# First unit's x made by products with parts of the identity instead of transfers, more warming products, and a new step plan

## The chip, the cores and the metric

The kernel runs on one core of one Trainium2 chip. The metric is the device time of one execution in microseconds (us); lower is better. Five engines matter: TensorE (PE, matrix products), VectorE (DVE), ScalarE (ACT), GpSimd (POOL) and SyncE (SP, which issues most transfers).

## The reference

A gated linear recurrence for every batch and head, followed by a two-layer network. All inputs of the recurrence are float32; `w_in` and `w_out` come out as float64, so the kernel receives them as pairs of 32-bit words.

```python
# q, k, v, f_logit: (4, 8, 768, 48)
f = 1 / (1 + exp(-f_logit))
for t in range(S):
    state = f[:, :, t, :, None] * state + einsum('bhd,bhe->bhde', k[:, :, t], v[:, :, t])
    y[:, :, t] = einsum('bhd,bhde->bhe', q[:, :, t], state)
x = y.transpose(0, 2, 1, 3).reshape(3072, 384)      # tokens by heads*dims
h = x @ w_in                                        # 384 x 2048
g = h * (1 / (1 + exp(-1.702 * h)))
out = g @ w_out                                     # 2048 x 384
```

## The kernel before

**Units.** The 3072 tokens are worked in twelve units of 256 tokens (three for each batch entry). For a unit the recurrence is solved in chunks of 64 tokens: f, q and k are loaded and turned so that head dimensions lie on partitions; six levels (block sizes 1 to 32) each make score products on PE (`score`, L448), multiply the q and k halves by running products of f in place on DVE (`promote`, L542 or L546), set a copy of K aside on ACT (`set_aside`, Kc, L517) and move the masked scores into the matrix A (`evacuate`, L489, L498, L508). The next level's score needs the Kc and the promoted q of the level before. Then K is turned (`turn_k`, tkn L621, kn L622), chunk states are formed (pd L669 on PE; L691 to L695 on DVE), y is summed in PSUM from A times v (`add`, L558) and from the states times q (L716), and the part "W" brings y to x.

**From y to x.** y lies in PSUM as 48 rows for each of two heads (partitions 0 to 47 and 64 to 111) and four head pairs. The network wants x with 128 of the 384 features on partitions, three such blocks. `half(h)` copies y into the tile yT on ACT (L731) and `to_x` moves it into xT by transfers (L781, L786): for units 0 and 1 the second half goes partly through ACT's queue, else all are on SP's. The first 96 features of each block are two heads of one pair; the last 32 of each come from the fourth pair.

**Network.** Units 0 and 1 work by `mlp_block`: for four of the sixteen 128-wide slices of the hidden layer at a time, four h steps (`mlp_h`, L1130, three products each, then the gelu on ACT into g, L1134) and eight o steps (`mlp_o`, L1144; summed by L1194 or L1196). Later units use other product schemes (L897, L1036). These steps form one list, `fill`, and each plan letter "f" emits the next one.

**Weights.** `pairs` holds sixteen pieces of weights. `fetch_weights` (L207) issues the transfer of a piece's words into one of three buffers (bits). `begin_pair` scales its high words on ACT in place (L239) and queues three DVE steps: low (L235), high (L228, which needs the scaled high words) and both (L238, the result into w_in or w_out). `convert` emits one queued step. A fetch reuses the buffer of the piece three before it. Piece numbers 0 and 1 are w_in, 2 and 3 w_out, and so on by fours. An h or o step stands in the list with the count of pieces that it needs done.

**Order.** Until the end of unit 2's plan every engine's order is the program's order, written by hand. `opening` does unit 0, and part of unit 1's loads and turns. Then `follow(n, fill, PLAN[n])` emits the parts of unit n in turn, and after each part the letters of its entry:

```text
f  next fill step          c  one convert step       p  begin the next piece
w  fetch a piece           s  a sum of weights       k  keep_up: one 128x320 product of the
HOLES: letters inside unit 2's levels                   identity with masks, result unused
```

The first part of unit 1 is composed: unit 0's part "W" (y L716 and then x), followed by unit 1's level 0. PE and DVE thus meet unit 0's y, its x, and then unit 1's first scores in this order. `bank` hands out four PSUM banks in turn to products that need one.

**Start.** A table load on ACT, the clearing of A on DVE (L121), then two warming products on the cleared A (L116), the POOL work for the identity and masks, and the turns of unit 0's f, k and q on PE (L379) with copies on ACT (L384).

Of the kernel before, what the change touches and what calls it, by code (L numbers as in the profile page):

```python
# [23 lines left out]
def kernel(  # L24
# [96 lines left out]
    nc.vector.memset(A, 0.0)  # L121
    nc.vector.memset(ones, 1.0)
    serial = count()
    flat_A = A.rearrange("p c f t -> p (c f t)")
    keep_up(2, 192, (flat_A[:, :P], flat_A[:, :192]))

    R = U // 32
    RW = R * D + HS - D
# [42 lines left out]
    D2, DR = 2 * D, P - 2 * D  # L171
    assert NP == NK + 1 and NK * DR == D2

    NGR = NFF // FG


# [14 lines left out]
    R_BY_ACT = range(0)  # L191
    fetched, todo = {}, []
    state = {"fetch": 0, "begin": 0, "done": 0, "behind": 0}

# [15 lines left out]
    def begin_pair(m):  # L210
# [14 lines left out]

        def high():
            t["s"] = tmp("s", 1).bitcast(I32)
            ve.tensor_scalar(t["s"], hi, 3, None, op0=ALU.logical_shift_left)  # L228

        def low():  # L230
            t["r"] = tmp("a", 2).bitcast(I32)
            if m in R_BY_ACT:
                nc.scalar.activation(t["r"], lo.bitcast(U32), AF.Copy, scale=2.0 ** -29)
            else:
                ve.tensor_scalar(t["r"], lo.bitcast(U32), 2.0 ** -29, None, op0=ALU.mult)  # L235
# [4 lines left out]
        if m in R_BY_ACT:  # L240
            low()
        else:
            todo.append(low)
        todo.extend((high, both, None))

    def begin_next():

        if state["begin"] < len(pairs):
            begin_pair(state["begin"])
            state["begin"] += 1  # L250

    def convert():
# [77 lines left out]
    def rows(h):  # L330
        return slice(h * HS, h * HS + D)
# [6 lines left out]
    def attention(n):  # L338
# [211 lines left out]
        def add():  # L550


            t["py"] = ps.tile([P, NG, NP, 2, HS], F32, tag="y", name=f"y_{n}")
            for a in range(NP):
                for f in (1, 0):
                    for h, g in TILES:
                        to, w = (slice(0, HS), HS) if h == g == 0 else (columns(h, g), D)
# [141 lines left out]
        def _():  # L699
# [614 lines left out]
    def opening():  # L1314

        begin_f, begin, begin_k, begin_gates = units[0][0]
        next_f, next_q, next_k, next_gates = units[1][0]
        level, evacuate, turn_k = units[0][2]
        load_raw(0, 0)
        load_raw(0, 2)  # L1320
        load_raw(0, 1, (nc.scalar,))
        fetch_weights()
        begin_f()
        begin_gates()
        begin_k()
        begin()
        load_raw(1, 0)
        load_raw(1, 2)
        load_v(0)
        load_raw(1, 1)  # L1330
        fetch_weights()
        fetch_weights()
        for l in range(NL):
            chosen[:] = [2, 3][l % 2:][:1]
            level(l)
            if l in (2, 3):
                next_f((0, 4)[l - 2:][:1])
            elif l < NL - 1:
                keep_up(1)
            if l == 1:  # L1340
                begin_pair(0)
                state["begin"] = 1

        nc.scalar.activation(q_end, q_end, AF.Gelu_apprx_sigmoid)
        chosen[:] = [2, 3]
        turn_k(0)
        turn_k(2)
        for l in range(NL - 1):
            evacuate(l)
            if l == 1:  # L1350
                units[0][3]()
        chosen[:] = [2, 3, 2, 3]
        next_q()
        begin_pair(1)
        state["begin"] = 2
        evacuate(NL - 1)
        units[0][1][-2][1]()
        next_gates()
        for _ in range(NOP):
            convert()  # L1360
        fetch_weights()

    fill = []
    opening()
    FIRST = 'k'
# [13 lines left out]
    fill += mlp_blocks((0, 0)) + mlp_blocks((0, 1))  # L1379
    fill += mlp_blocks((1, 0), (1, 1)) + mlp_blocks((0, 2), (1, 2)) + mlp_blocks((0, 3), (1, 3))  # L1380
    follow_steps(FIRST)
    follow(1, fill, PLAN[1])
    chores += [*sums_of_w(("c3", "p15", "c2", "p6"))]
    follow(2, fill, PLAN[2])
    assert state["fetch"] == len(pairs)
    fill_order.close()
    assert state["done"] == 2 * len(pairs) or moe_w_in.dtype == F32
    while chores:
        chores.pop(0)()
    for n in range(N_FILL, NALL):  # L1390
# [46 lines left out]
```

## Time and profile before

| | |
|---|---|
| three runs | 585.39, 586.55, 587.39 us; median 586.55 |
| profiled execution | 586.86 us; its span 585.1 us, first to last instruction |
| busy: PE, DVE, ACT, POOL | 566.7, 442.3, 289.3, 141.7 us |
| keep-up and warming products (L116) | 28 instructions |
| first h product of the network (L1130) | 40.48 us from the span's start |
| transfers into xT for unit 0 | issued 34.20 to 37.58 us |
| unit 1's y products (L716) | start at 64.16 us |

Every matrix product in float32 shows as two matmul instructions. All later times in a trace count from the start of the span. The rest of the device time, 1.76 us, lies outside the span.

### The profile page before, as it was taken

The numbers are of one execution on the slowest core, as the hardware profiler recorded it, in microseconds if no ns is written. First come the engines' busy times: TensorE is split into PE (matmuls) and PEld (weight loads), VectorE is DVE, ScalarE is ACT, GpSimd is POOL, SyncE is SP. The second block draws the span as 40 slices with busy tenths as digits, with TensorE's granted clock in tenths as the row PEclk, the third lists the DMA queues.
The fourth block names the chain that finished last, engine by engine and source line by source line (L and its number), as shares of the span: only waits on it lengthen the run. The fifth ranks groups of instructions, "written<-read, shape, count | busy, mean of one in ns | idle before, by whom it ended". The sixth has DMA issues, their size and how long they took to land.

```text
span 585.1 us, 18537 instructions
## 1 busy us (share of the span) xinstructions
PE 566.7 (97%) x7838; PEld 516.1 (88%) x7838; DVE 442.3 (76%) x697; ACT 289.3 (49%) x588; POOL 141.7 (24%) x226
## 2 busy tenths in 40 slices
PE   7989899999999999999999999999999999999997
PEld 6757676776889999999999999999999999998896
DVE  1899887996888886997786897786897786461284
ACT  4755544322543563663563563564563563552440
POOL 3030120605442601501501601502502503103000
DMA  7869695932453362362443353452451211001000
GB/s 184 192 167 240 151 258 132 241 79 71 104 137 75 103 148 59 97 154 68 122 117 69 93 135 89 111 128 59 120 130 43 64 39 29 29 2 30 26 1 29
DMA packets 86772, 60.34 MB, mean 103 GB/s; under 512 B 33505, under 2 KB 78465, under 8 KB 86689
## 3 DMA queue, kind: packets, MB, share of 16 engines
q1 hardware_dynamic: 86208, 58.57, 40.2%
q8 instruction: 62, 1.02, 0.7%
q10 hardware_dynamic: 481, 0.59, 0.4%
q14 instruction: 21, 0.17, 0.1%
HBM read 45.49 MB, written 8.91 MB: 93 GB/s over the span
## 4 chain that ended last, share of the span: by engine, by line
PE 67%; DVE 12%; DMA 9%; ACT 5%; SPq 3%; issue 2%; POOL 0%; ACTq 0%; DVEq 0%; POOLq 0%
PE h L1036 14%; PE o_Y L897 12%; PE o_Z L897 9%; PE sc L448 6%; PE h_y L1036 5%; PE o_X L897 5%; DMA bits<-in_moe_w_in_dram 4%; PE o_W L897 4%; PE h L1130 3%; PE o L1144 3%; DVE X L367 2%; PE y L716 2%; DMA raw<-in_q_dram 2%; PE sc L669 2%; DVE z L629 2%
## 5 line engine op out<-in xcount | busy, mean ns | idle before, releaser
L546 DVE TENSOR_TENSOR X<-X,tot 128x1024 f32<-128x1024 f32 x50 | 67.2, 1345 | 45.3 <-PE sc L448 37.4
L517 ACT COPY Kc<-X 128x512 f32<-128x512 f32 x72 | 48.2, 670 | 86.2 <-DVE X L546 66.2
L998 POOL TENSOR_TENSOR E<-xT 128x128 f32<-128x128 f32 (+1 forms) x36 | 17.1, 484 | 228.0 <-DMA xT<-yT 228.0
L1130 PE MATMUL h<-xT,w_in 128*128 128x256 f32 x288 | 66.1, 383 | 3.8 <-DMA xT<-yT 2.9
L1130 PEld LDWEIGHTS h<-xT,w_in 128*128 128x128 f32 x288 | 53.5, 190 | 14.0 <-issue 4.0
L1036 PE MATMUL h<-E,w_in 128*128 128x128 f32 (+1 forms) x476 | 62.8, 277 | 0.6 <-DVE g L1064 0.6
L1036 PEld LDWEIGHTS h<-E,w_in 128*128 128x128 f32 x476 | 57.4, 192 | 1.5 <-issue 0.9
L897 PE MATMUL o_Y<-T,S 128*128 128x192 f32 x320 | 57.7, 329 | 0.0
L1066 ACT ACTIVATE g<-g 128x512 f32<-128x512 f32 (+1 forms) x70 | 40.3, 589 | 28.3 <-DVE g L1064 28.2
L897 PEld LDWEIGHTS o_Y<-T,S 128*128 128x128 f32 x320 | 52.2, 190 | 0.6
L1064 DVE TENSOR_TENSOR g<-g,h 128x512 f32<-128x512 f32 (+1 forms) x58 | 35.9, 638 | 16.3 <-PE h L1036 14.8
L367 DVE STREAM_TRANSPOSE X<-raw 128x512 f32<-128x512 f32 x40 | 42.9, 1111 | 3.1 <-PE y L716 2.7
L1144 PE MATMUL o<-w_out,g 128*128 128x384 f32 x128 | 43.7, 491 | 0.1
L508 DVE COPY_PREDICATED A<-masks,sc 128x256 f32<-128x256 uint32 (+1 forms) x98 | 41.8, 504 | 0.1
L1144 PEld LDWEIGHTS o<-w_out,g 128*128 128x128 f32 x128 | 23.7, 190 | 14.8 <-issue 0.2
L731 ACT COPY yT<-y 48x256 f32<-48x256 f32 (+1 forms) x66 | 21.1, 370 | 29.3 <-PE y L716 28.9
L394 POOL TENSOR_SCALAR F<-F 128x1024 f32<-128x1024 f32 x10 | 12.3, 1228 | 87.6 <-ACT F L397 87.6
L1055 ACT ACTIVATE g<-h 128x512 f32<-128x512 f32 (+1 forms) x52 | 28.5, 576 | 9.6 <-PE h L1036 9.3
L448 PE MATMUL sc<-X,Kc 48*64 48x64 f32 x1344 | 28.1, 220 | 2.7 <-ACT Kc L517 1.1
L448 PEld LDWEIGHTS sc<-X,Kc 48*64 48x64 f32 x1344 | 24.0, 134 | 6.9 <-ACT Kc L517 3.1
L897 PE MATMUL o_X<-w_out,g 128*128 128x192 f32 x160 | 29.6, 331 | 0.5 <-ACT o_X L861 0.5
L1134 ACT ACTIVATE g<-h 128x256 f32<-128x256 f32 x48 | 17.2, 383 | 24.9 <-PE h L1130 24.7
(161 smaller groups left out, 1201.8 us busy)
## 6 DMA issues: line engine op xcount, KB each, us to landing
bits<-in_moe_w_out_dram SPq DMA_DIRECT2D x8, 768.0 KB
raw<-in_f_logit_dram SPq DMA_DIRECT2D x48, 96.0 KB
raw<-in_k_dram SPq DMA_DIRECT2D x48, 96.0 KB
bits<-in_moe_w_in_dram SPq DMA_DIRECT2D x8, 576.0 KB
raw<-in_q_dram SPq DMA_DIRECT2D x44, 96.0 KB
k_tok<-z SPq DMA_DIRECT2D x64, 64.0 KB
kt<-k_tok SPq DMA_DIRECT2D x16, 256.0 KB
out_dram<-osb SPq DMA_DIRECT2D x20, 192.0 KB
```

Source lines behind the costliest of these rows:

```text
L367: nc.vector.transpose(view(out, at, [[HALF, NP], [step, R4], [R4 * step, 32]]), by_half[:, j, f].rearrange("p a (j d) -> p (a j) d", j=R4) ...
L448: nc.tensor.matmul(t["sc"][h][g * HS:(g + 1) * HS, a, s, :], lhsT=t["Kc", l][rows(h), x:x + HS], rhs=rhs(h, a, g), start=True, stop=True,)
L508: moved = nc.vector.copy_predicated(out=view(A, c * HALF + at, dims), mask=mask.bitcast(U32), data=got)
L517: nc.scalar.copy(c.rearrange("p (n two m) -> p n two m", two=2, m=m), view(X, KF * SLOT, [[2 * m, SLOT // (2 * m)], [(KR - KF) * SLOT + m, ...
L546: nc.vector.tensor_tensor(x, x, y, ALU.mult)
L897: nc.tensor.matmul(t[name], lhsT=lhs(f), rhs=rhs(f), start=(new and i == 0), stop=(i == HF - 1), skip_group_check=True,)
L1036: nc.tensor.matmul(ph[:, t], lhsT=WA[a][:, f // 2, f % 2 * P:(f % 2 + 1) * P], rhs=E[n][b], start=(root and t == 0), stop=not goes_on, ski ...
L1055: nc.scalar.activation(to, ph, AF.Copy, scale=float(sign))
L1064: copied["sum"] = nc.vector.tensor_tensor(to, to, part, ALU.add if sign > 0 else ALU.subtract)
L1066: nc.scalar.activation(to, to, AF.Gelu_apprx_sigmoid)
L1130: nc.tensor.matmul(ph, lhsT=w_in[:, ff // 2, c, ff % 2 * P:(ff % 2 + 1) * P], rhs=xTs[n][:, c, :], start=(c == 0), stop=(c == NK - 1))
L1144: nc.tensor.matmul(t["po"], lhsT=g[ff // FG][:, ff % FG, tt * P:(tt + 1) * P], rhs=w_out[:, ff, :], start=(ff == ffs[0]), stop=(ff == ffs[ ...
```

## The change

1. **Start.** The warming products go from two to six, and the clearing of A is split: the 192 columns that they read first, the rest behind them.
2. **Parts of the identity.** The unused place of `w_out[:, 15, :128]` first holds `select`, two groups of identity columns copied by POOL: heads' rows 0 to 47 and 64 to 111 side by side (96 columns), and 32 columns for the middle block.
3. **Unit 0's x.** y of unit 0 is placed so that a head's rows stay the same for both token groups (`columns`, `add`). Two copies (one per direction f) bring 112 rows of y into yT; three pairs of products with `select` or `ident` (96 and 32 rows of output) write x into two PSUM banks; two copies bring them into xT. No transfer is left for unit 0.
4. **Plan.** New letters: "a" begins a piece whose low word is scaled by ACT instead of DVE, "i" a small product of the identity with itself. "f" now converts until its piece is done, "w" does nothing where no buffer is due, and a begin fetches a piece that isn't fetched. The conversion of piece 0 is spread over the opening. PLAN and HOLES are new; the opening's places for letters are listed in `PLAN[0]`.

```diff
-    nc.vector.memset(A, 0.0)
+    serial = count()
+    WARM = 6
+    flat_A = A.rearrange("p c f t -> p (c f t)")
+    nc.vector.memset(flat_A[:, :192], 0.0)
+    keep_up(WARM, 192, (flat_A[:, :P], flat_A[:, :192]))
+    nc.vector.memset(flat_A[:, 192:], 0.0)
     nc.vector.memset(ones, 1.0)
-    keep_up(2, 192, (flat_A[:, :P], flat_A[:, :192]))
...
+    select = w_out[:, NFF - 1, :P]
+    nc.gpsimd.tensor_copy(select[:, :D2]..., view(ident, 0, [[HS, 2], [1, D]]))
+    nc.gpsimd.tensor_copy(select[:, D2:]..., view(ident, DR, [[DR, 2], [1, DR // 2]]))
...
-    HOLES = {(N_FILL, 0): "ccp", (N_FILL, 1): "cwcc", (N_FILL, 2): "cwp", (N_FILL, 3): "cc", (N_FILL, 4): "cw"}
+    HOLES = {(N_FILL, 0): "wc", (N_FILL, 1): "ckccc", (N_FILL, 2): "fcp", (N_FILL, 3): "cc", (N_FILL, 4): "pwcw"}
...
         def columns(h, g):
-            return rows(h ^ g)
+            return rows(h ^ g if n else h)
...
+            if not n:
+                for f in (1, 0):
+                    at, step = (0, 1) if f else (U - 1, -1)
+                    nc.scalar.copy(
+                        view(yT[:HS + D], at, [[U, NP], [step * HS, NG], [step, HS]]),
+                        py[:HS + D].rearrange("p g a f t -> p f a g t")[:, f],
+                    )
+                to = [bank([P, 2, U], "x_0"), bank([P, 1, U], "x_1")]
+                for c in range(NK):
+                    pt = to[c // 2][:, c % 2]
+                    y = yT[:HS + D].rearrange("p a g t -> p a (g t)")
+                    nc.tensor.matmul(pt[:D2], lhsT=select[:HS + D, :D2], rhs=y[:, c], start=True, stop=True)
+                    rest = (ident[:HS + D, :DR], select[:HS + D, D2:], ident[:HS + D, HS + DR // 2:HS + D])[c]
+                    nc.tensor.matmul(pt[D2:], lhsT=rest, rhs=y[:, NK], start=True, stop=True)
+                    if c:
+                        nc.scalar.copy(xT[:, 2 * c - 2:c + 1, :], to[c // 2])
+                xTs[n] = xT
+                return
...
             if step == "f":
-                assert fill[0][2] <= state["done"], (fill[0], state)
+                while fill[0][2] > state["done"]:
+                    convert()
                 fill.pop(0)[1]()
...
+            elif step == "a":
+                begin_next(True)
+            elif step == "i":
+                keep_up(1, P, (ident, ident))
             elif step == "w":
-                fetch_weights()
+                if state["fetch"] < min(len(pairs), state["done"] // 2 + PAIRS_AHEAD):
+                    fetch_weights()
...
     PLAN = {
         3: (
-            "fffffffsffsf", "fsffsffsf", "f", "fsfsfsffsfsfsf", "", "ffff", "ff", "ffffffffffffffffsffsf", "fffsf",
+            "fcfffffffff", "sfsffsfsfsf", "", "fsffsffssfsfsf", "", "fffff", "fffffff", "fffffffffffsfffspfa",
+            "fffs",
         ),
+        0: (
+            "ik", "k", "kpc", "ck", "k", "", "", "k", "", "", "", "", "", "", "", "", "", "", "ckw",
+        ),
         1: (
-            "cccwcccwkkkkk", "kkkcf", "cfccwf", "fcffcwffcffcf", "ffcc", "f", "cwc", "fcc", "ffcf", "pw", "fw", "ff",
+            "pcccckkwccwff", "f", "kcfccccwf", "ffcfwfkfccf", "ffcc", "f", "wcwc", "ccf", "ffcf", "", "fw", "ff",
             "fffffff",
         ),
         2: (
-            "ffff", "ffffffff", "fcfcfcwffcfcfcwfffcfcfcff", "sss", "fcfcfcfffffss", "fcfcfcffffffff", "",
-            "fffffffffff",
+            "ffff", "fffffffff", "fcfccfwffcffcpfccfcwfcffa", "sss", "fcffcfffcffss", "fafccfffffffafff", "p",
+            "ffffffffff",
         ),
     }
```

In the opening the letters of `PLAN[0]` stand behind the turns of f (entry 1), the products of f and the turns of k (2), the turns of q (3), each of the six levels (4 to 9), the turning of K (10), the moves of five levels (11 to 15), unit 1's q (16), the last move (17), the states (18) and unit 1's products of f (19). Before, there were keep-ups behind levels 0, 1 and 4, `begin_pair(0)` behind level 1, `begin_pair(1)` behind unit 1's q, and three convert steps, a fetch and a keep-up at the end.

More of the change, by code (lines that the diff above doesn't have):

```diff
@@ L172 @@
     assert NP == NK + 1 and NK * DR == D2
+    select = w_out[:, NFF - 1, :P]
+    nc.gpsimd.tensor_copy(select[:, :D2].rearrange("p (h d) -> p h d", h=2), view(ident, 0, [[HS, 2], [1, D]]))
+    nc.gpsimd.tensor_copy(select[:, D2:].rearrange("p (h d) -> p h d", h=2), view(ident, DR, [[DR, 2], [1, DR // 2]]))
     NGR = NFF // FG
@@ L190 @@
     NOP = 3
-    R_BY_ACT = range(0)
     fetched, todo = {}, []
@@ L244, in begin_pair, with begin_next @@
         todo.extend((high, both, None))
-    def begin_next():
+    def begin_next(by_act=False):
         if state["begin"] < len(pairs):
-            begin_pair(state["begin"])
+            if state["fetch"] == state["begin"]:
+                fetch_weights()
+            begin_pair(state["begin"], by_act)
             state["begin"] += 1
@@ L556, in add @@
                     for h, g in TILES:
-                        to, w = (slice(0, HS), HS) if h == g == 0 else (columns(h, g), D)
+                        to, w = (slice(0, HS), HS) if h == 0 and (not n or g == 0) else (columns(h, g), D)
                         nc.tensor.matmul(
@@ L1337, in opening @@
                 next_f((0, 4)[l - 2:][:1])
[L1338 to L1342, printed above, removed]
+            follow_steps(next(places))
         nc.scalar.activation(q_end, q_end, AF.Gelu_apprx_sigmoid)
@@ L1351, in opening @@
                 units[0][3]()
+            follow_steps(next(places))
         chosen[:] = [2, 3, 2, 3]
         next_q()
-        begin_pair(1)
-        state["begin"] = 2
+        follow_steps(next(places))
         evacuate(NL - 1)
+        follow_steps(next(places))
         units[0][1][-2][1]()
+        follow_steps(next(places))
         next_gates()
-        for _ in range(NOP):
-            convert()
-        fetch_weights()
+        follow_steps(next(places))
     fill = []
-    opening()
-    FIRST = 'k'
     PLAN = {
         3: (
-            "fffffffsffsf", "fsffsffsf", "f", "fsfsfsffsfsfsf", "", "ffff", "ff", "ffffffffffffffffsffsf", "fffsf",
+            "fcfffffffff", "sfsffsfsfsf", "", "fsffsffssfsfsf", "", "fffff", "fffffff", "fffffffffffsfffspfa",
[3 more added lines that the diff above has]
+            "ik", "k", "kpc", "ck", "k", "", "", "k", "", "", "", "", "", "", "", "", "", "", "ckw",
         ),
         1: (
-            "cccwcccwkkkkk", "kkkcf", "cfccwf", "fcffcwffcffcf", "ffcc", "f", "cwc", "fcc", "ffcf", "pw", "fw", "ff",
+            "pcccckkwccwff", "f", "kcfccccwf", "ffcfwfkfccf", "ffcc", "f", "wcwc", "ccf", "ffcf", "", "fw", "ff",
             "fffffff",
@@ L1380 @@
     fill += mlp_blocks((1, 0), (1, 1)) + mlp_blocks((0, 2), (1, 2)) + mlp_blocks((0, 3), (1, 3))
-    follow_steps(FIRST)
+    opening()
     follow(1, fill, PLAN[1])
@@ L1384 @@
     follow(2, fill, PLAN[2])
-    assert state["fetch"] == len(pairs)
+    while state["done"] < 2 * len(pairs):
+        convert()
     fill_order.close()
-    assert state["done"] == 2 * len(pairs) or moe_w_in.dtype == F32
     while chores:
```

14 lines of the change are left out of this document (9 added, 5 removed).

## The prediction

> **What bounds the kernel now.** I read the busy shares first, then who TensorE (PE) waits for, then the opening on PE and VectorE (DVE) in order of time, because the diff touches only the opening and the step plans of units 1 to 3. Line 1 of the page and the longest of PE's waits:
>
> ```profile
> PE 566.7 (97%) x7838; PEld 516.1 (88%) x7838; DVE 442.3 (76%) x697; ACT 289.3 (49%) x588; POOL 141.7 (24%) x226
> ```
> ```profile
> PE h L1130 <- DMA xT<-yT: 2.9, 2, 1.8
> PE idle L116 <- DVE A L121: 2.0, 1, 2.0
> PE sc L448 <- ACT Kc L517: 1.1, 2, 0.8
> ...
> PE h L1130 <- ACT g L1134: 0.8, 1, 0.8
> ...
> PE sc L448 <- DVE A L508: 0.6, 1, 0.6
> ```
>
> PE is the bound. It has 18.4 us of idle, and busy time that is worth nothing: the keep-up products "idle" (L116). The opening shows both, as does the timeline of PE:
>
> ```profile
> 2.02 1.65 PE L116 MATMUL idle<-A 128*128 128x192 f32 x4 [2.02 <-DVE A L121]
> 4.47 8.32 PE L379 MATMUL t<-ident,raw 128*64 128x128 f32 x96 [0.81 <-DMA raw<-in_q_dram]
> ...
> 31.64 1.04 PE L716 MATMUL y<-X,st 48*48 48x64 f32 x46 [0.22 <-ACT y L680]
> ...
> 33.15 2.96 PE L116 MATMUL idle<-masks,ident 128*128 128x320 f32 x10
> 36.90 0.71 PE L448 MATMUL sc<-X,Kc 48*64 48x64 f32 x32 [0.79 <-ACT Kc L517]
> 37.53 1.88 PE L116 MATMUL idle<-masks,ident 128*128 128x320 f32 x6
> 40.48 1.88 PE L1130 MATMUL h<-xT,w_in 128*128 128x256 f32 x6 [1.06 <-DMA xT<-yT]
> 42.29 0.69 PE L448 MATMUL sc<-X,Kc 48*64 48x64 f32 x32
> ```
>
> Unit 0's y ends at 32.7; its first product h starts at 40.48. Between them PE does two score products of unit 1 (L448) and eight keep-ups. From 40.48 on it is dense. The remaining idle before 130 us is 1.83 at 69.5 (unit 1's xT transfers), 0.35 at 77.4 (Kc), 0.60 at 83.8 (L508) and 0.81 at 127.7 (g).
>
> DVE in the same stretch does the weight conversion (L235, L228, L238) between unit 1's levels (L542):
>
> ```profile
> 30.43 1.32 DVE L235 TENSOR_SCALAR a<-bits 128x768 int32<-128x768 uint32 x1
> ...
> 33.64 1.42 DVE L542 TENSOR_TENSOR X<-X,F 128x512 f32<-128x512 f32 x2
> 34.98 0.68 DVE L489 TENSOR_TENSOR A<-sc,masks 128x512 f32<-128x512 f32 x1
> 35.58 0.55 DVE L235 TENSOR_SCALAR a<-bits 128x768 int32<-128x768 uint32 x1
> ```
>
> It has no idle time from 30.4 to 50.6: while x travels, DVE converts pairs 1 and 2 and finishes unit 1's level 0. That cover is what the change disturbs.
>
> **The start.** The clearing of A before the warming products is cut from 1024 to 192 columns (0.91 us, so about 0.25), and they start near 1.3 instead of 2.02. There are twelve instructions instead of four. They follow one another by 0.32 us, so they end near 5.3, after the raw f that PE waited for at 4.47. The turns L379 ran slowly first and fast later, with the granted clock (PEclk, third from the end) at 1.00 in both stretches of the windows view, PE's busy time and count standing ahead:
>
> ```profile
> 4.50:10.00 5.50, 5.50 (x52) 5.50 (x54) 1.00 0.92 236
> 10.50:12.50 2.00, 2.00 (x40) 2.00 (x38) 1.00 0.90 207
> ```
>
> That is 0.106 us an instruction, then about half (0.055 between starts); the change of pace came 5.8 us into the unbroken work that began at 4.47. If unbroken work from 1.3 does the same, it comes at 7.1: 17 turn instructions at 0.106, 79 at 0.055, and three keep-ups between them (0.23, 0.56, 0.56 by L116's 0.28 an instruction) end at 12.75 instead of 12.6. The last two ScalarE copies then start without the queue of before (X 12.53 to 13.73 behind Kc), so level 0 starts at about 13.65 instead of 13.79: -0.15. [...] The two POOL copies that make the parts of the identity fall into POOL's idle time from 3.3 to 8.9; nothing hides them if F came earlier, and then they cost under 1 us of POOL.
>
> [...]
>
> **x by products.** Removed: six transfers (34.20 to the wait that ended at 40.44), their issues on SP (3.3 us) and ScalarE (1.2). Added: two copies of 112x512 out of PSUM (kn L622, 128x512, follow one another by 0.48 and take 0.59: 1.1 in all), twelve matmul instructions of 256 columns, two copies of 512 and 256 columns, the last of which run beside PE. Unit 0's y now uses two parts of the array where four were used: +0.2. Twelve instructions at h L1130's 0.2155 make 2.6. Lower end 1.45, if the 96- and 32-row parts run side by side as the two halves of L379 do (128 columns in 0.055 an instruction). Upper end 3.85: the step from L1130 to L448 came 0.10 late at 42.29 and the way back 0.25 in sum, so five changes of shape cost 0.5 to 1.25. I take 3.1, since 96 rows are nearer to L1130's 128. [...]
>
> So copies end at 34.0 and products at 37.1. The program keeps PE's order: unit 1's level-0 score, at 32.52 before, is queued behind the products and starts at 37.05. So DVE, which needs that score for its second L542, idles from about 32 to 37.7, and all of pair 1 and pair 2's conversion stands behind it in the plan ("pcccckkwccwff").
>
> **Unit 1.** From that score, by rows: score 0.65, L542 0.62, L489 0.60, two pairs of conversion at 0.47+0.50+0.88, L542 0.62 and Kc 0.7: level 2's score starts about 7.0 after level 0's, at 44.05 (42.29 before), with PE idle for 0.6 despite two keep-ups (0.56 each). DVE stays full. Going on the same way (third keep-up, five conversion steps, a wait of some 0.75 for pair 3's w_out, fourth keep-up), level 4's score comes 15.5 after, at 52.55 (52.34), with eleven fill steps done in both. DVE is then late for the turning of K (0.55 of PE idle), and unit 1's y L716 starts 28.0 after, at 65.05 against 64.16. PE's own work alone from score to y is 40.48 to 64.16 plus two scores (1.26) and four keep-ups (2.24), 27.2: even a full PE would bring 64.25. So x arrives three us earlier and nothing is left: +0.9, from -0.75 (products 1.45) to +1.65 (3.85). Pair 3's bits are issued at 28.6 instead of 32.7, and there are no x transfers beside them, so no transfer is late. The 1.83 at 69.5 stays, as it is unit 1's own transfer after its y with six o steps over it in both plans.
>
> **Unit 2 and after.** Before, ScalarE's Kc at 77.01 was queued behind the scaling of pair 9, whose bits landed at 76.14; that step is moved behind Kc: -0.35. One h goes between level scores (-0.60 at 83.8), and one keep-up is added there (+0.56). One more h goes ahead of unit 2's states, which covers the 0.81 at 127.7. Of the "a" steps only one finds a pair to begin, pair 14; its low word leaves DVE (1.16 at 114.79, on a full queue) for ScalarE (0.9, which idled 6.3 there). Weights fetched later in unit 2 are needed only from 97.3 on. Sum -1.2, from 0 to -1.76. Unit 3's plan has the same count of fill steps and its PE does not wait between 130 and 160: 0.
>
> **Sum.** Profiled execution 586.86 (span 585.1 and 1.76 around it): -0.15 +0.9 -1.2 = 586.4. It lay 0.31 above the median of the runs; against the median 586.55 that is 586.1.
>
> **Rivals.** [...] (2) DVE's backlog: products take 3.85, the score comes at 37.8, y L716 at 65.8 (+1.65), and the backlog enters unit 2's transposes (L367), so no gap there closes and the keep-up adds 0.56: 586.55 - 0.15 + 1.65 + 0.56 = 588.6. It decides once the score starts after 37.8. For it: no idle time is left on DVE. Against: before, DVE waited 5.5 us for scaled bits in unit 1 and 2, slack that can absorb it. (3) The plan does not do what it says: the start gains nothing and unit 2's gaps stay open while unit 1 comes out even: 586.55 to 587.4.
>
> **Numbers.** Forecast with its near surroundings 0.46 (its own range 584.8 to 587.6), rival 1 0.28, rival 2 0.18, rival 3 0.08. About 0.3% (1.76 us) is what a measurement of this kernel can tell from no change. Rival 1 and the forecast's lower tail (0.04) are faster, rival 2 and the upper tail (0.03) slower: 0.32, 0.47, 0.21. The range takes in both outer rivals: 582.8 to 588.7.
>
> **What would show it.** In the changed profile: the pace of L379 changes near 7; level 0 starts near 13.65; twelve select products last 3.1; unit 1's first score starts near 37 and DVE shows an idle stretch of some 5 us ended by PE; first h near 38.8; unit 1's y L716 near 65; PE's waits for Kc, L508 and g before 130 are gone, and one of 1.8 for xT is left. I am wrong if DVE is not idle there, if PE waits under 1 us from 37 to 65, or if the time moves elsewhere, after 165.

## The result and the profile after

The changed kernel takes 595.95 us (median of 594.52 to 597.59) where the kernel before takes 586.64 in the same runs: a ratio of 1.0162, 95% interval 1.0130 to 1.0194. That is 9.3 us slower; the forecast was 586.1 with a range up to 588.7. The profiled execution, the slowest of the four, took 597.59, its span 595.62 (before: 585.07). Start times from the two traces show where the 10.55 arise:

| start of | before | after | added in this stretch |
|---|---|---|---|
| unit 0's level 0 (first score) | 13.79 | 14.07 | +0.28 |
| unit 0's y | 31.64 | 32.38 | +0.46 |
| unit 1's first score | 32.52 | 42.43 | +9.17 |
| unit 1's y | 64.16 | 72.02 | -2.05 |
| unit 2's y | 135.22 | 146.07 | +2.99 |
| end of the span | 585.07 | 595.62 | -0.30 |

So two places lose, units 0 to 1 and unit 2, and nothing moves after that. The page of after, PE's busy line and the granted clock over 40 slices:

```profile
PE 576.1 (97%) x7860; PEld 519.9 (87%) x7860; DVE 440.0 (74%) x697; ACT 289.3 (49%) x587; POOL 139.7 (23%) x228
PEclk9979999999999999999999999999999999999999
```

PE is busy 9.4 us longer with 22 more instructions, and the clock has a dip in the third slice. The mean clock of the four executions was 0.989 to 0.994. An estimate from these means, with all that was lost taken as lost at the 0.50 of this trace, is (1 - clock) x 2 x span: 0.991 makes 10.7 us at half clock, and the four lie between 7 and 13; where the other three had them is not shown. PE's waits in after:

```profile
PE o L1170 <- ACT kn L629: 3.2, 1, 3.2
PE h L1156 <- DMA xT<-yT: 1.9, 1, 1.9
PE x L744 <- issue: 1.3, 1, 1.3
PE y L723 <- issue: 1.2, 1, 1.2
...
PE t L386 <- issue: 1.0, 1, 1.0
```

Before had neither the first nor any "issue" wait of that size. "issue" is time for which the profile names no releaser. The two places, on PE's timeline of after:

```profile
27.28 1.20 PE L386 MATMUL t<-ident,raw 128*64 128x128 f32 x17
29.51 1.09 PE L386 MATMUL t<-ident,raw 128*64 128x128 f32 x15 [1.04 <-issue]
...
32.38 1.54 PE L723 MATMUL y<-X,st 48*48 48x64 f32 x46
35.15 0.27 PE L723 MATMUL y<-X,st 48*48 48x64 f32 x2 [1.23 <-issue]
36.68 0.64 PE L744 MATMUL x<-yT,w_out 112*96 112x256 f32 x2 [1.26 <-issue]
37.26 1.06 PE L746 MATMUL x<-yT,ident 112*32 112x256 f32 x2
...
41.44 1.06 PE L746 MATMUL x<-yT,ident 112*32 112x256 f32 x2
42.43 1.14 PE L455 MATMUL sc<-X,Kc 48*64 48x64 f32 x32
...
45.78 3.59 PE L1156 MATMUL h<-xT,w_in 128*128 128x256 f32 x12
```

PE stops in the middle of the turns (29.51) and of unit 0's y, with two of its products left (35.15). Counted over all of PE's instructions, weight loads and the sequencer's own included, the stops lie at 961 and 1217, 256 apart, and each ends 2.4 to 2.7 us after a transfer of 16384 bytes began on the instruction queue (26.82 and 32.71): I read them as PE waiting for its own code. The third wait, 1.26 ahead of the products, is for ScalarE's two copies of y into yT (35.51 to 36.58), which those late products of y had held up. From 33.9 to 36.7 PE therefore did almost nothing, and then the granted clock fell to 0.50. In the windows view (PE busy first, granted clock third from the end):

```profile
37.00:42.00 5.00, 5.00 (x12) 1.34 (x10) 0.00 (x0) 0.58 (x1) 0.00 (x0) 0.52 0.02 3
42.00:47.50 5.50, 5.50 (x43) 3.82 (x42) 3.84 (x7) 2.55 (x4) 0.00 (x0) 0.50 0.10 10
47.50:52.00 4.50, 4.50 (x79) 3.49 (x77) 3.78 (x7) 1.66 (x4) 0.00 (x0) 1.00 1.01 265
```

The clock's record is 0.50 from 37.22 for 10.24 us. The twelve select products took 36.68 to 42.43, 5.75 us. Unit 1's first score is queued behind them, and VectorE waits for that score, as its timeline shows:

```profile
32.45 1.09 DVE L549 TENSOR_TENSOR X<-X,F 128x512 f32<-128x512 f32 x1
43.63 0.69 DVE L549 TENSOR_TENSOR X<-X,F 128x512 f32<-128x512 f32 x1 [10.09 <-PE sc L455]
```

The second place is ScalarE in unit 2 (first two groups of lines from ScalarE's timeline, the last from PE's):

```profile
117.93 0.90 ACT L244 ACTIVATE bits<-bits 128x768 f32<-128x768 f32 x1 [5.25 <-DMA bits<-in_moe_w_out_dram]
118.71 0.91 ACT L238 ACTIVATE a<-bits 128x768 int32<-128x768 uint32 x1
119.50 1.07 ACT L404 ACTIVATE F<-F 128x1024 f32<-128x1024 f32 x1
120.44 0.59 ACT L629 COPY kn<-tkn 128x512 f32<-128x512 f32 x1
```
```profile
121.08 1.56 PE L1170 MATMUL o<-w_out,g 128*128 128x384 f32 x4 [3.22 <-ACT kn L629]
```

The letter "a" at the end of unit 2's third entry begins piece 14, whose bits SP had issued only at 112.67. ScalarE stands at its first scaling until 117.93, and the low word, the gates' sigmoid and the copy of kn are queued behind it; PE waits 3.22 for that copy.

### The profile page after: what moved, and what is told of

It reads as the page before. It is cut to its first block, busy times and chain, and to the rows that moved or that the text cites. A ratio compares the mean times of both kernels' runs of the same rounds, so it can differ in the third digit from the quotient of the medians.

```text
span 595.6 us, 18581 instructions
## 1 busy us (share of the span) xinstructions
PE 576.1 (97%) x7860; PEld 519.9 (87%) x7860; DVE 440.0 (74%) x697; ACT 289.3 (49%) x587; POOL 139.7 (23%) x228
## 3 DMA queue, kind: packets, MB, share of 16 engines
q8 instruction: 62, 1.02, 0.8%
## 4 chain that ended last, share of the span: by engine, by line
PE 79%; DVE 9%; DMA 4%; ACT 4%; issue 2%; SPq 2%; ACTq 0%; DVEq 0%
PE h L1062 14%; PE o_Y L923 12%; PE h L1156 9%; PE o_Z L923 8%; PE sc L455 6%; PE h_y L1062 5%; PE o L1170 5%; PE o_X L923 5%; PE o_W L923 4%; PE y L723 2%; PE t L386 2%; PE idle L116 2%; DVE X L553 2%; PE sc L676 2%; PE y L565 2%
## 5 line engine op out<-in xcount | busy, mean ns | idle before, releaser
L1156 PEld LDWEIGHTS h<-xT,w_in 128*128 128x128 f32 x288 | 54.7, 192 | 13.1 <-DMA xT<-yT 2.5
L757 ACT COPY yT<-y 48x256 f32<-48x256 f32 (+1 forms) x60 | 19.1, 368 | 28.0 <-PE y L723 27.7
L923 PE MATMUL o_W<-T,g 128*128 128x192 f32 x160 | 29.5, 331 | 0.0
```

The lines of the kernel that those rows point to most:

```text
L923: nc.tensor.matmul(t[name], lhsT=lhs(f), rhs=rhs(f), start=(new and i == 0), stop=(i == HF - 1), skip_group_check=True,)
L1156: nc.tensor.matmul(ph, lhsT=w_in[:, ff // 2, c, ff % 2 * P:(ff % 2 + 1) * P], rhs=xTs[n][:, c, :], start=(c == 0), stop=(c == NK - 1))
```

## The experiments

My theories after the result: (1) ends of code pieces, moved by the added PE instructions, stop PE and drop the clock; (2) the products stand ahead of unit 1's score, so VectorE idles; (3) piece 14 is begun too early. The rival to all: the products, or the plan, simply cost what was seen. All times below are of each run's profile, except the medians and ratios (95% intervals, to the kernel before on the same chip).

| run | median | ratio | level 0 | unit 0's y | first score | unit 1's y | unit 2's y | span |
|---|---|---|---|---|---|---|---|---|
| e1 four keep-ups ahead of the products | 593.55 | 1.0116 (1.0080 to 1.0151) | 13.33 | 34.73 | 42.95 | 71.33 | 144.03 | 592.95 |
| e2 "a" two entries later | 592.88 | 1.0112 (1.0084 to 1.0140) | 13.58 | 34.85 | 41.23 | 69.61 | 139.93 | 589.07 |
| e3 after with transfers | 593.36 | 1.0126 (1.0083 to 1.0168) | 13.65 | 35.09 | 37.39 | 70.13 | 144.75 | 594.44 |
| e4 before with products | 592.30 | 1.0102 (1.0081 to 1.0123) | 12.76 | 30.61 | 36.86 | 66.09 | 139.95 | 589.81 |
| e5 before + 8 short products | 589.45 | 1.0061 (1.0028 to 1.0093) | 15.58 | 34.91 | 35.78 | 66.10 | 138.44 | 587.91 |
| e6 after with the old start | 594.10 | 1.0125 (1.0108 to 1.0143) | 13.55 | 32.68 | 38.92 | 67.32 | 143.13 | 593.62 |
| e7 e1, e2 and e6 together | 591.68 | 1.0073 (1.0050 to 1.0095) | 12.31 | 30.58 | 37.69 | 66.08 | 136.43 | 586.18 |
| e8 e7, conversion filling VectorE's idle time | 590.43 | 1.0057 (1.0042 to 1.0072) | 13.66 | 31.59 | 38.71 | 67.89 | 139.57 | 588.60 |
| e9 before with unit 2's and 3's plan of e2 | 585.15 | 0.9984 (0.9968 to 0.9999) | 13.41 | 31.28 | 32.15 | 63.13 | 135.14 | 583.78 |
| e10 before + 16 short products | 592.04 | 1.0128 (1.0096 to 1.0159) | 19.36 | 37.22 | 38.09 | 69.83 | 140.87 | 590.13 |
| e11 after, piece 14's low word on VectorE | 593.21 | 1.0126 (1.0098 to 1.0153) | 13.88 | 34.78 | 41.48 | 69.87 | 141.95 | 590.94 |
| e12 e1, products in order of shape | 594.19 | one run | 13.75 | 34.58 | 42.26 | 70.64 | 143.10 | 592.39 |
| e13 e2, weight fetches later in the program | 588.22 | one run | 13.60 | 31.93 | 38.17 | 66.57 | 136.88 | 586.29 |
| e14 e9 with four warming products | 585.87 | 0.9980 (0.9963 to 0.9997) | 12.42 | 31.43 | 32.30 | 62.55 | 135.11 | 583.84 |
| e15 e9, products behind the score | 589.96 | 1.0054 (1.0034 to 1.0074) | 13.98 | 31.82 | 33.10 | 66.37 | 139.85 | 588.49 |
| e16 e2, weight fetches behind v | 590.12 | one run | 14.21 | 32.19 | 38.43 | 66.83 | 138.88 | 588.26 |
| e17 e12, weight fetches behind v | 591.16 | one run | 13.33 | 31.70 | 38.23 | 66.63 | 139.70 | 589.34 |
| e18 e14, one weight fetch behind v | 584.01 | 0.9964 (0.9951 to 0.9977) | 12.25 | 30.09 | 30.96 | 61.27 | 131.62 | 580.66 |

**Products, clock and order (e1, e3, e4, e12, e15).** e1 puts `keep_up(4)` ahead of the banks `to`, to fill PE's wait while yT is copied.

> The changed kernel with four keep-ups between unit 0's y products and its x products. Theory 1 (idle array): the gap of TensorE there (33.9 to 36.7) lets the granted clock fall to 0.50 from 37.2 to 47.5; with work in the gap the clock stays 1.00, the x products take about 2.7 instead of 5.8, unit 1's y products start near 67.5 instead of 72.0, time about 591.5. Theory 2 (products in the queue): the products and VectorE's late start are the loss whatever the clock does; time 595 to 597.

e12 takes e1 and makes one loop of the 96-row products and a second one of the 32-row ones:

```diff
+                for c in range(NK):
                     rest = (ident[:HS + D, :DR], select[:HS + D, D2:], ident[:HS + D, HS + DR // 2:HS + D])[c]
```

> The kernel after with four keep-ups between y and x of unit 0 (products at full clock 3.4 us), and the six select products in order of shape: three of 96 rows, then three of 32. Theory (a change of shape costs, as the prediction took from L1130 and L448: 0.10 to 0.25 each, and four of five changes go): the twelve instructions take 2.4 to 3.0. Rival (the 0.28 an instruction is that of the shape, whatever came before): 3.3 to 3.5 as before. The total says nothing here: within 1.5 us of 593.5.

PE's timelines of e1 and then of e12:

```profile
39.56 0.60 PE L745 MATMUL x<-yT,w_out 112*96 112x256 f32 x2
40.09 0.62 PE L747 MATMUL x<-yT,ident 112*32 112x256 f32 x2
40.64 0.67 PE L745 MATMUL x<-yT,w_out 112*96 112x256 f32 x2
...
42.95 0.70 PE L455 MATMUL sc<-X,Kc 48*64 48x64 f32 x32
```
```profile
39.45 1.46 PE L745 MATMUL x<-yT,w_out 112*96 112x256 f32 x6
40.84 0.62 PE L749 MATMUL x<-yT,ident 112*32 112x256 f32 x2
41.30 0.59 PE L749 MATMUL x<-yT,w_out 112*32 112x256 f32 x2
...
42.26 0.71 PE L455 MATMUL sc<-X,Kc 48*64 48x64 f32 x32
```

At full clock the products take 3.39 us from first start to the score, and 2.81 in order of shape: starts 0.2155 apart within a shape, as h's, so four changes of shape cost 0.58, 0.15 each. So the changes of shape are most of what lifts 2.6 to 3.4, each inside the prediction's 0.10 to 0.25. In after the same twelve took 5.75, so half clock is worth 2.4 of them. e1's own total (593.55) came between its two expectations; its profile has stops of 2.85 in the opening and 0.84 within unit 0's y.

e4 puts the products alone into the kernel before, e3 takes them out of after.

> The kernel before with unit 0's x by products and nothing else (old start, old plan with its eight keep-ups behind the scores). Theory 1 (idle array): the gap between y and the products is still empty, the clock falls, 591 to 593. Theory 2 (products in the queue, at full clock 2.6 to 3.9): unit 1 is late by 1 to 2, 587.5 to 588.5. If the products pay: below 585.

> The changed kernel with unit 0's x by transfers, as before, and the new plan kept. Theory 1 (idle array): TensorE has two keep-ups for a wait of about 6 us, so the clock falls here too; about 594 to 597. Theory 2 (products in the queue): without the products VectorE is on time, first h near 40.8, unit 1's y products near 65.5; about 589.

Unit 0's y to unit 1's y takes 32.52 before, 35.48 with the products alone (e4, full clock there), 35.04 with the new plan alone (e3), 39.64 in after and 36.60 in e1. These are not parts that add up: e3 had a stop of 1.20 and, behind a wait of 3.58 for xT, a dip of its own (twelve h instructions in 4.51, e1 2.75), e1 its stop and the time of its keep-ups. The clean measure is in four profiles that have the products and the new plan, but no stop between unit 0's y and the products (e2, e6, e13, e16). They take 34.64 to 34.76. PE's timeline of e13:

```profile
31.93 1.54 PE L723 MATMUL y<-X,st 48*48 48x64 f32 x48
34.74 0.64 PE L744 MATMUL x<-yT,w_out 112*96 112x256 f32 x2 [1.27 <-POOL tot L446]
38.17 0.70 PE L455 MATMUL sc<-X,Kc 48*64 48x64 f32 x32
```

The wait of 1.27 is that for ScalarE's copies, which ended at 34.64 (POOL's last tot had ended at 34.45). It is as long as in after, and nothing covers it. Of seven profiles with this wait and no keep-ups in it (after, e2, e4, e6, e11, e13, e16) the clock fell behind it only in after, where the stop of 1.23 came on top. From y to the score e13 needs 6.24 (after: 10.05), from the score to unit 1's y 28.40 (after: 29.59). So products and plan by themselves lose 2.1 against before, and 5.0 of after's 7.12 came with the stop and the half clock. Five other profiles with transfers and unit 1's old first entries (e5, e9, e10, e14, e18) take 31.12 to 32.61, so the 2.1 can be 2.0 to 3.6; no profile shows a gain by the products.

e3's median of 593.36 fits neither of its expectations. e4's 592.30 is the figure of theory 1, but not by its reason, since the clock did not fall at its products. It lost again at unit 1's xT, 3.53 instead of 1.83: an SP transfer at 71.68 waited for the semaphore of one that ScalarE had issued at 69.30. Half clock for 3.41 from 76.38 then slowed the h steps behind it, 7.13 instead of 5.44.

e15 takes e9 (described below: before with the mended plan of units 2 and 3), and places the products behind unit 1's score, in the place of keep-ups, with the copies into xT behind level 1's Kc:

> Kernel e9 with x of unit 0 by products, but placed behind unit 1's first score instead of ahead of it, in order of shape, in the place of five keep-ups; the two copies into xT behind level 1's Kc on ScalarE; three more keep-ups taken out ahead of the first h. Theory (in the change the products lost because unit 1's score and with it VectorE waited for them): first score at 32.2 as in e9, VectorE's idle time there under 1 us, products 2.7 at full clock, first h at 38 to 39 (39.3 in e9), 583.5 to 585.3. Rival (products lose by themselves: the wait for the two copies of y, the clock behind it, or the ends of code pieces): first h at 41 or later, 587 to 589.

The score came at 33.10 and the products at full clock, but x was no earlier. PE's timeline of e15, then ScalarE's:

```profile
41.55 2.93 PE L1157 MATMUL h<-xT,w_in 128*128 128x256 f32 x6 [2.61 <-ACT xT L749]
```
```profile
40.40 0.62 ACT L523 COPY Kc<-X 128x512 f32<-128x512 f32 x1 [4.26 <-DVE X L548]
40.92 0.85 ACT L749 COPY xT<-x 128x512 f32<-128x512 f32 x2
```

The copies into xT stood behind a Kc copy that waited 4.26 for VectorE. The time (589.96) is above the rival's range, by a mechanism that neither theory had: my own order on ScalarE. Whether products can win with another order there stays open.

**Unit 2 (e2, e11, e9).**

```diff
-            "ffff", "fffffffff", "fcfccfwffcffcpfccfcwfcffa", "sss", "fcffcfffcffss", ...
+            "ffff", "fffffffff", "fcfccfwffcffcpfccfcwfcff", "sss", "afcffcfffcffss", ...
```

> The changed kernel with the letter a moved from the end of unit 2's third entry to the head of its fifth, so that piece 14's scaling stands behind the first copy of the turned K on ScalarE. Theory 3 (ScalarE's order): the scaling waits for its transfer (until 117.9) with that copy behind it; moved, TensorE's wait of 3.2 for the copy is gone and the time is about 592.7. Rival (VectorE's full queue in unit 2 is the loss): 595 to 596.

The wait for kn is gone, unit 1's y to unit 2's y takes 70.32 instead of 74.05, and the median is 3.07 lower (the two intervals just overlap): theory 3 holds. e11 asks whether the place or the low word on ScalarE was at fault ("a" replaced by "p" at the old place):

> The kernel after with piece 14 begun at the same place, but its low word on VectorE as for the others. Theory (the place is at fault: ScalarE's scaling of the high word still waits there for bits that land near 118, ahead of the copy of kn): the PE wait for kn only shrinks by the low word's 0.9, from 3.2 to about 2.3; 595.0, 594.5 to 595.8. Rival (the low word on ScalarE is at fault): the wait is gone, as with the later place, about 592.9.

The wait is gone there too (593.21, the rival's figure), but in part by luck. ScalarE still stood until 114.86 for the bits, though SP had issued them at 110.01. With the low word, e1, e3, e6, e12 and e17 still show 1.2 to 3.3 of the wait. The nearest is e12: bits issued at 110.33, scaled from 114.94, the copy of kn at 117.48 where e11 has 116.64, and 1.62 of the wait left. So the low word is worth 0.84 of it. The rest was hidden in e11 because PE came 0.93 later to these products (114.67 against 113.74): half clock from 77.79 had slowed its h steps. The place, with the time at which the bits land, remains the greater part. e9 puts the mended plan of units 2 and 3 on the kernel before, with its own start, transfers and first entries of unit 1:

> The kernel before, with only the new plan from the end of unit 1 on (unit 1's last letters, unit 2's letters and holes, unit 3's letters; the piece with its low word on ScalarE begun where its bits have landed). Start, opening and unit 0's transfers are as before, so PE's instructions up to unit 1's y keep their places. Theory (the loss is made by what shifts PE's instructions and by the order from unit 0 to unit 1; unit 2's plan by itself is a gain of the size of the prediction's term): 584.8 to 586.0, PE's waits for Kc and L508's A near 77 and 84 gone, y of unit 2 starts 70.3 after y of unit 1 (71.1 before). Rival (the new plan of unit 2 also only moves the waits, to the transfers of unit 1's x or to the ends of code pieces further on): 586.6 to 588.5, a new PE gap over 0.8 between 100 and 165.

585.15, by the ratio 0.94 below before (0.06 to 1.87), and the waits at 77 and 84 are gone. But unit 1's y to unit 2's y took 72.01 and not the 70.3 that I expected: half clock for 3.41 from 70.72 stretched its h steps from 5.44 to 7.11. Four profiles with the mended plan and full clock there (e2, e7, e13, e18) take 70.31 to 70.35, 0.7 less than the 71.06 of before. The prediction's term for unit 2 (-1.2, 0 to -1.76) thus had the right sign, with 0.7 us in this stretch and 0.94 in the whole; the change spoiled it by one letter.

**The start and PE's code (e5, e10, e6, e7, e8, e13, e14, e16, e17, e18).** e5 and e10 add `keep_up(8, 32, ...)` and `keep_up(16, 32, ...)` behind the two warming products of before.

> The kernel before with eight short products (32 columns) behind the two warming ones, in the wait for the raw f: as many TensorE instructions more as the new start and its keep-ups have, and hardly any time. Theory 4 (code): TensorE's instructions arrive in pieces of 16,384 bytes, so that more instructions ahead move the ends of the pieces to other work, where TensorE stands for up to 2.9 us; 587.5 to 589.5, with a gap released by nothing before 40 us. Rival (the count does not matter): 586.0 to 586.8.

> The kernel before with sixteen short products (32 columns, result unused) behind the two warming ones, where eight gave 589.45. Theory (the added products cost nothing themselves; they shift the ends of the 256-instruction pieces of PE's code, by 64 instructions here against 32, to other work): no doubling of the loss; 586.6 to 589.5, gaps without a releaser at instruction counts 705, 961 or 1217 again, at other times than with eight (705 about 22 instead of 24.4). Rival (each added product costs its share, by a later start): twice the loss of eight, about 592.3, with level 0 later by twice as much and no gap at those counts.

e5's number came, and a stop of 1.19 at count 705 with it. e10 takes most of that reading away: 592.04, as its rival said, with one stop of only 0.33. The opening of e10 on PE's timeline:

```profile
2.02 8.32 PE L116 MATMUL idle<-A 128*128 128x192 f32 x36 [2.02 <-DVE A L121]
10.27 8.09 PE L380 MATMUL t<-ident,raw 128*64 128x128 f32 x96
19.36 0.70 PE L449 MATMUL sc<-X,Kc 48*64 48x64 f32 x32 [1.00 <-ACT X L385]
```

The short products were not free: 0.213 us apart, they delayed the turns by 5.80, and after 6.8 us of them (8.3 with the warming products) the turns were still slow. Their pace changed at 15.66 (11.57 in e5, 10.29 before). Level 0 came 5.57 later and the median 6.24: here the delay of the start passed to the end about one for one. Of e5's 2.9, 1.79 was that delay, and only the rest can be the stop.

> The changed kernel with the start of before (two warming products, A cleared in one piece, no keep-ups between the turns), conversion of piece 0 left early. Theory 4 (code, by the new start's instructions): the gaps at 22.5, 28.5 or 34 go or move, 592 to 594. If the new start gains by its earlier pace: 596 to 597.

> The changed kernel with the letter a later, four keep-ups between unit 0's y and x, and the old start. If the three act apart: 595.95 less 3.1, 2.4 and 2 to 3 (start) is 587.5 to 588.5. If the gaps stand in for each other: 590 to 592. Against before it tells what the products cost with all else mended (theory 2: 1 to 3 above 586.3).

> The kernel of the run before this one with piece 1 converted ahead of unit 0's y, in VectorE's idle stretch, pieces 2 and 3 behind unit 1's levels 1 and 2, and the four keep-ups behind unit 1's scores left out. Theory 2 (VectorE's late start behind the products): y of unit 1 about 2 earlier than in that run, 584.5 to 586.5. Rival (TensorE's own order is the bound by then): within 0.7 of it.

In e6 `WARM` is 2 and the keep-ups between the turns are gone; its median is 1.85 below after's, with overlapping intervals. e7 gives 591.68, the figure of its second expectation. Its profiled execution, the fastest (588.01), has no stop, no wait for kn and full clock, and still needs 35.50 from unit 0's y to unit 1's y, 0.86 more than e13 because of its four keep-ups. e8 fills VectorE's idle stretch with piece 1's conversion, leaves out the keep-ups behind unit 1's scores and takes off 1.25, less than expected: PE waits 1.23 for ScalarE ahead of unit 0's y, 1.45 for VectorE's w_out, and 3.14 for unit 1's xT.

In e1, e2, e3, e11 and e12 PE stopped for 2.0 to 2.85 us at count 705 in the opening, as in e2:

```profile
21.84 0.68 PE L455 MATMUL sc<-X,Kc 48*64 48x64 f32 x28 [0.17 <-DVE X L549]
25.37 0.48 PE L455 MATMUL sc<-X,Kc 48*64 48x64 f32 x4 [2.85 <-issue]
```

The transfer of that piece of code began 4.4 to 5.1 us after PE had entered the piece before it (count 449), against 1.1 to 3.7 in the other profiles. PE needs 4.8 to 5.6 us for a piece there, and resumes 2.7 to 3.0 after the transfer's start. e13 moves the opening's two `fetch_weights()` behind unit 0's levels, e16 and e17 behind unit 1's v:

> Kernel e2 (a later), with the two weight fetches of the opening (pieces 1 and 2, 1.5 MB) moved from ahead of unit 0's levels to behind them. Read at one place: PE's gap without a releaser at instruction count 705 (2.85 in e2 at 22.5, 2.0 to 2.85 in five of six profiles with the new start), and the time from level 0 to unit 0's y (21.3 in e2, 17.85 before). Theory (the piece of code waits behind data in busy DMA engines, 92% of them busy from 16 to 26): the gap is under 0.8 and level 0 to y is 18.0 to 19.0. Rival (the gap hangs on where the pieces end in PE's program, not on other traffic): 2 or more and about 21. The total says nothing: pieces 1 and 2 land some 6 us later and stall VectorE after that.

> Kernel e2 with the two weight fetches of the opening behind unit 1's v on SP, where SP itself waits till some 26 (moving them behind the levels in program order, in e13, had changed nothing: SP ran ahead and issued them at 18.63, as in e2 at 18.32). Read at one place: piece 705 of PE's code. Theory (its fetch, asked for when the piece before is entered near 17.5, waits behind the 1.5 MB of weights in the DMA engines): the fetch starts by 19.0, no gap over 0.3 at 705, level 0 to unit 0's y 18.0 to 18.6. Rival (the fetch's delay has nothing to do with these transfers): it starts between 20 and 23 as in six of the seven profiles with the new start, with a gap of 2 or more if it starts after 22. The total says nothing, since the weights come 8 us later.

> The same edit on kernel e12, as a second sample of the same place (e12's own profile: fetch at 22.23, gap 2.30, level 0 to unit 0's y 20.8). Theory: fetch by 19.0, no gap over 0.3 at 705, 18.0 to 18.6. Rival: fetch between 20 and 23, and a gap of 2 or more if after 22.

e13's edit moved no transfer: SP runs ahead and issued the weights at 18.63 (18.32 in e2). Yet the code's transfer began at 19.72, no stop came at 705 (one of 0.89 at 961), and the one run took 588.22. The same order of transfers gives both outcomes, so the stop depends on the execution too. In e16 and e17 the weights left at 27.75 or later. Windows of e2 and then e16 (DMA share is the last but one):

```profile
16.00:26.00 10.00, 6.74 (x165) 4.95 (x166) 5.66 (x10) 5.06 (x10) 0.00 (x0) 0.96 0.92 227
```
```profile
16.00:26.00 10.00, 9.35 (x232) 7.44 (x233) 8.90 (x19) 6.50 (x14) 0.00 (x0) 1.00 0.38 81
```

The transfer of code began 2.3 and 2.8 after the piece before was entered, later than my "by 19.0" and inside the rival's 20 to 23, but neither had a stop, and level 0 to unit 0's y took 17.98 and 18.37 (21.27 in e2, 20.83 in e12). Two runs without a stop, where five of the seven profiles with the new start and weights in that stretch had one, speak for the traffic, but don't prove it: before, with a DMA share of 0.94 in the same window, had no stop either. Nor is it shown that added instructions move the stops, as theory 1 has it: in every profile with a stop of 0.8 or more it lies at 705, 961 or 1217.

e14 is e9 with `WARM = 4` and the split clearing, without keep-ups between the turns; e18 moves the second opening fetch behind v:

```diff
-        fetch_weights()
         fetch_weights()
...
-            ..., "", "p", "", "", "cccwk",
+            ..., "", "p", "", "w", "cccwk",
```

> Kernel e9 (before with the plan from unit 1's end on) with the change's start alone: four 192-column warming products from about 1.15 on instead of two from 2.02, the clearing of A split; no keep-ups between the turns. Theory (wide products bring the clock up, 4.7 to 6.5 in the kernels with six of them against 9.2 to 10.3 with two, and four end before the raw f arrives): the granted clock is full by 7.3, level 0 starts at 12.3 to 12.9 (13.4 in e9), and the gain passes to the end: 584.2 (583.5 to 584.8). Rival (eight more instructions move the ends of PE's code pieces into the opening): a gap over 0.8 at count 705 or 961 and 585.5 to 588.

> Kernel e14 (before with the plan from unit 1's end on and four wide warming products) with the second of the opening's two weight fetches (0.77 MB) behind unit 1's v on SP. Theory (the gain of the earlier clock, 1 us at level 0, was lost in e14 to a gap of 1.77 at count 961, and such gaps come with the weights' traffic): the gap is gone or under 0.8, unit 0's y at 30.3 to 30.8 instead of 31.4, and 584.2 to 585.3, below the kernel before by 0.2 to 0.35%. Rival (the gap stays, or VectorE waits for the later piece 2): 585.5 to 587.

PE's timeline of e14, then of e18:

```profile
29.27 0.38 PE L382 MATMUL t<-ident,raw 128*64 128x128 f32 x2 [1.77 <-issue]
```
```profile
1.15 2.93 PE L116 MATMUL idle<-A 128*128 128x192 f32 x8 [1.15 <-DVE A L124]
4.68 6.57 PE L382 MATMUL t<-ident,raw 128*64 128x128 f32 x96 [0.60 <-DMA raw<-in_f_logit_dram]
12.25 0.70 PE L451 MATMUL sc<-X,Kc 48*64 48x64 f32 x32 [0.99 <-ACT X L387]
...
30.09 1.04 PE L719 MATMUL y<-X,st 48*48 48x64 f32 x46 [0.21 <-ACT y L683]
```

In these two the clock was full at 6.03 and 7.01; with the old start it was full between 7.23 (e7) and 10.51 (e15), a wider spread than the 9.2 to 10.3 of my expectation. Both reach level 0 about 1.0 earlier than the seven profiles with the old start, which lie between 12.31 (e7) and 13.98, 13.35 in the mean. e14 lost it to a stop at count 961; e18's profile, of the fastest of seven executions (582.44), has none, and the median is 584.01, 0.23 to 0.49% below the kernel before and faster than both kernels of this case. It keeps the transfers for unit 0's x.

## Why the prediction was wrong

- **Start, -0.15: +0.28.** The pace changed at 6.57 (the record of full clock begins at 6.50), near the forecast 7. But the turns ended at 13.25, not 12.75: keep-ups between the turns took 0.95 and 0.74 where I had 0.79 and 0.56, and the turns 6.27 where I had 6.15, more than the earlier pace returned. Nine profiles with the new start have level 0 at 13.71 in the mean, seven with the old one at 13.35. In the two profiles without those keep-ups (e14, e18) level 0 lies 1.0 earlier. The lower end of the range, 582.8, counts a gain of 1.2 at the start, which no run of this start shows: level 0 came at 13.33 (e1, e17) to 14.21 (e16) in the nine, from 0.46 ahead of the 13.79 of before to 0.42 behind it.
- **"If unbroken work from 1.3 does the same": half right.** Unbroken work is not enough: e10's narrow products ran for 6.8 us and left the turns behind them at half pace. From the start of unbroken work to the change of pace it took 5.8 us before, 5.4 in after (from 1.15), at most 3.9 in e2, whose turns ran at full pace from 5.04 on (32 in 1.97), and 13.6 in e10 (from 2.02). No single length fits these four.
- **Products, 3.1 (1.45 to 3.85): 5.75.** At full clock 3.39, inside the bounds. What failed is that I priced them at full clock and put PE's stops, which the page of after calls "issue" and before did not show, at nothing. They are the first step of the loss: 1.04, 1.23, then the clock. In e13, with the same uncovered wait for the copies but without the second stop, the products took 3.43. Unit 0's y on two parts of the array took 1.54 instead of 1.11, so its +0.2 was half of what it cost.
- **First score at 37.05, VectorE idle some 5 us ended by PE: 42.43 and 10.09.** The mechanism was right, but mis-sized: the copies ended at 36.58 instead of 34.0, and the products took 5.75 instead of 3.1. "It decides once the score starts after 37.8" was rival 2's point, and it was passed by 4.6 us; its price, 588.6, was too low, because it too had full clock and no stop.
- **Unit 1, +0.9: +7.86 by unit 1's y.** The working behind the score was nearly right: 28.0 from the first score to unit 1's y by forecast, 28.40 in e13, and 29.59 in after, where half clock lasted 5 us into it. The way to the score failed: from unit 0's y 5.41 by forecast, 6.24 in e13 and 10.05 in after. Without stop and half clock the term would have been 2.1 (e13 against before), still above the +1.65 of its range; e4, with the old plan, has +2.96.
- **Unit 2, -1.2 (0 to -1.76): +2.99.** That piece 14's low word leaves DVE for ScalarE, "which idled 6.3 there", looked at the engine's idle time and not at its queue: what is queued behind the begin on ScalarE, and whether the bits have landed. That is the step that failed, worth 3.07 in the median and 3.73 in this stretch (e2). "Weights fetched later in unit 2 are needed only from 97.3 on" hid it: the bits were needed by the instruction ahead of kn's copy. Kc's and L508's waits went as forecast; g's did not (1.2), though the forecast had a fill step cover it. Without the bad letter the plan is worth -0.7 in this stretch (e2, e7, e13, e18) and -0.94 in the whole (e9, 0.06 to 1.87).
- **Unit 3, 0:** unit 2's y to unit 3's y took 43.21 instead of 43.78, and what follows 0.27 more.

## What to carry to other kernels

An engine that idles is no free place for an instruction that waits on a transfer (ScalarE stood 5.25 us for piece 14's bits here, and PE 3.22 for the copy behind them): read what stands behind it in that engine's queue and when the bytes land. When PE work is inserted, look also at what fills PE just ahead of it, since 2.5 idle microseconds there were followed by 10 us at half clock here, and at who waits for the products that it now precedes. A start delayed by 5.57 us cost 6.24 at the end here, and a test that adds "free" work to the start measures that first.

## What the runs showed of the hardware

- PE stopped for up to 2.85 us at instruction counts 256 apart (705, 961, 1217), and went on 2.2 to 3.0 after a transfer of 16384 bytes began on the instruction queue. The page of after has 62 such transfers (queue 8, 1.02 MB), and its trace 15,893 instructions of PE by the same count, 256 for each. Why the transfer begins 1.1 us after the piece before is entered in one execution and 5.1 in another stays open.
- One idle stretch of 1.93 us (e9, unit 1's xT) was followed by half clock for 3.41 us; the same wait in e18 was not. In after, 2.5 us of idle time with 0.27 of work inside brought 10.24 at half clock, three times 3.41, although PE was busy throughout it. Why the clock stayed at half while PE was busy is not shown.
